# A gated linear attention and a feed-forward layer on one core: one hand-written order of 1,096 steps replaced by another

## The chip, the cores and the metric

The kernel runs on one core of one Trainium2 chip. A core has a matrix engine (TensorE, PE in the profile; its weight loads are PEld), three engines for elementwise work (VectorE or DVE, ScalarE or ACT, GpSimd or POOL) and a queue that issues transfers (SyncE, SP). Each engine runs its own instructions strictly in the order in which they were listed, and waits where an instruction's data or buffer is not ready. [...] The metric is the device time in microseconds (us) of one execution, smaller being better.

## What is computed

Attention with a decaying state over 4 batches x 8 heads, 768 tokens, head size 48, and then a feed-forward layer over the 3072 tokens of 384 features, with 2048 hidden features:

```python
for t in range(S):
    state = alpha[:, :, t, :, None] * state + np.einsum('bhd,bhe->bhde', k[:, :, t], v[:, :, t])
    y[:, :, t] = np.einsum('bhd,bhde->bhe', q[:, :, t], state)
...
x = np.ascontiguousarray(attn_out.transpose(0, 2, 1, 3)).reshape(B * S, H * D)
...
h = x @ w_in
r = np.maximum(h, 0.0)
g = s * (r * r) + b
return (g @ w_out).astype(np.float32)
```

## The kernel before

The tokens are cut into 24 blocks of 128 (6 for each batch, numbered 0 to 23). A block goes through a fixed row of steps. Each step is a small Python function that records a few instructions on one engine, and a step's name with the block's number, such as `amat 13`, names it in this document:

- `load x n`, `load_w x w` (SyncE): one of the inputs q, k, v, a(lpha) for a block, or for a pair of blocks (0 to 5 come in pairs w = 0, 1, 2). The input buffers hold 8 blocks.
- `ln` (ScalarE), `cum` (TensorE), `ex` (ScalarE): logarithm of alpha, its running sum over the tokens, and the exponentials of the sum and of its negative.
- `km`, `qm` (VectorE): k and q times those exponentials. Then their transposes: for blocks 0 to 7 by `tr` (TensorE, n and 0 for q or 1 for k) and a copy out of PSUM, `cph` or `cp`; for the pairs from 8 on by a transposing transfer, `trd` (SyncE).
- `amat` (TensorE): the products of k and q inside the block, into the two banks `a_ps`; `am` (VectorE): the causal mask on both.
- `vcast`: v in bf16. `ya` (TensorE): masked products times v. `yi` (TensorE): q times the state from the earlier blocks, added into the same bank. `yev`: the result out of PSUM.
- `sp` (TensorE), `t1` (VectorE), `sd` and `sc`: the block's own part of the state, its sum with the carried state, and the sum decayed, once as the operand of the next block's `yi` (`sd`, two instructions) and once as the next carry (`sc`, POOL). From block 6 on the decay factors come through two small transfers, `last_row` and `decay`.
- `xt`, `xev` (up to block 17) or `xtd` (transfer, from 18 on): y transposed, the left operand of the feed-forward layer.
- `mp n u` (TensorE, 12 matmuls): quarter u of the hidden features, into one of the two banks `h_ps`; `rl` (ScalarE): the maximum with 0; `sq` (VectorE): the square.
- `o n u` (TensorE, 4 matmuls): quarter u of the sum for the output, into `o_ps`; `oev`: out of PSUM; `add_bias` (VectorE, blocks 0 to 12, kept in the space of the `w_in` staging) and `store` (SyncE).

The weights come as four transfers each, `load_w_in` and `load_w_out`, and are cast to bf16 by twelve `win i kk e` and five `wout`. `colsum`, `bias_sum` and `bias_row` make the constant row that b adds. `busy 256` is a matmul on constants into `o_ps`, whose result is not used; 78 of them stand in the opening.

Where a step can run on several engines, its last letter says which: a is ScalarE, v VectorE, p POOL (GpSimd); `sd` with s runs on VectorE and reads PSUM directly. The order of everything is one string, `order`, of 1,096 such steps; a loop at the end of the kernel calls them one by one. Nothing plans or reorders behind it: the listing, engine by engine, is the program. A step's place in the listing thus sets what it queues behind on its own engine, and each engine runs ahead of the others as far as data and buffers let it. Banks are handed out in the listing's order too: `mp`, `xt` and two of the `cum` take turns on the two banks of `h_ps`.

The helper that most engine letters go through, and the one for `sd`:

```python
def copy(eng, out, in_):
    if eng == "a":
        nc.scalar.activation(out=out, in_=in_, func=AF.Copy)
    else:
        (nc.vector if eng == "v" else nc.gpsimd).tensor_copy(out=out, in_=in_)
...
(nc.gpsimd if eng == "p" else nc.vector).tensor_tensor(
    out=sd_sb[n % 2][r, :, d], in0=src[r, :, d], in1=bl[r].to_broadcast([48, NP, 48]), op=ALU.mult
)
```

The lines of the profile: L148 and L142 loads, L154 and L159 weights, L198 fillers, L207 `ln`, L227/L230/L241 `cum`, L251/L252 `ex`, L273 `km`, L281 `qm`, L299 `tr`, L343 `amat`, L351 `am`, L366 `yi`, L382/L392 `ya`, L408/L417 `sp`, L432 `xt`, L457/L459 `t1`, L469 `sd`, L475 `sc`, L500 `mp`, L514 `rl`, L521 `sq`, L536 `o` (L564 for block 23), L553/L573 `oev` with the bias, L588 `add_bias`. L313 (ScalarE) and L315 (VectorE, POOL) are the helper `copy`, so `vcast`, `cph`, `yev`, `xev`, `win` and `oev` share them.

Of the kernel before, what the change touches and what calls it, by code (L numbers as in the profile page):

```python
# [14 lines left out]
def kernel(  # L15
# [628 lines left out]
    def win(i, kk, eng):  # L644
# [15 lines left out]
        busy 256; busy 256; busy 256; load_w k 1; busy 256; busy 256; busy 256; km 0; busy 256; busy 256; busy 256;  # L660
        busy 256; busy 256; busy 256; tr 0 1; busy 256; tr 0 0; load_w q 1; busy 256; busy 256; ex 1; km 1; cph 0 0 a;
        busy 256; busy 256; load_w_in 1; load_w_in 0; busy 256; cph 0 1 v; tr 1 1; ln 3; amat 0; cph 1 1 a; qm 1; tr 1 0;
        busy 256; busy 256; busy 256; busy 256; am 0; vcast 1 a; spread; ln 2; cum 2; cph 1 0 a; amat 1; cum 3; load_w v 1;
# [11 lines left out]
        sq 1 0; sq 0 2; ln 5; xev 3 a; tr 4 1; tr 4 0; cp 4; mp 1 3; wout 0 2 v; mp 0 3; rl 1 3; mp 3 3; cum 5; rl 0 3;
        mp 3 0; rl 3 3; ex 5; sd 3 v; wout 2 4 v; o 0 0; wout 4 8 a; o 1 0; wout 8 12 a; colsum 1; km 5; load k 6; tr 5 1;
        qm 5; tr 5 0; sq 2 2; cp 5; o 2 0; sq 1 3; masks; o 2 1; sc 3; rl 3 0; sq 2 3; o 1 1; wout 12 16 v; o 1 2; ln 6;
        load a 7; o 2 2; o 2 3; colsum 2; o 1 3; oev 2 a; sq 3 3; colsum 3; mp 3 1; cum 6; load k 7; sq 3 0; vcast 5 p;
        oev 1 a; amat 4; mp 3 2; load q 7; vcast 6 p; ex 6; o 0 1; o 0 2; rl 3 1; load a 8; sq 0 3; am 4; amat 5; o 0 3;
        qm 6; tr 6 0; sq 3 1; km 6; tr 6 1; load v 7; vcast 4 a; ya 4; am 5; cp 6; yi 4; ya 5; ln 7; sp 4; oev 0 a; sp 5;  # L680
        t1 4; cum 7; yev 4 a; xt 4; xev 4 v; amat 6; am 6; rl 3 2; sq 3 2; ex 7; mp 4 1; rl 4 1; qm 7; o 3 0; mp 4 3;
        mp 4 2; ln 8; sd 4 v; tr 7 0; load a 9; rl 4 3; load v 8; km 7; ya 6; yi 5; yev 6; yev 5 v; tr 7 1; cp 7; sq 4 3;
        rl 4 2; mp 4 0; load q 9; o 3 1; cum 8; rl 4 0; last_row 6; sq 4 0; amat 7; am 7; xt 6; load a 10; o 3 2; vcast 7 a;
        sp 6; xt 5; load q 8; load k 8; ln 9; ex 8; o 3 3; oev 3 v; sq 4 1; load k 9; xev 6; t1 6; km 8; decay 6; cum 9;
# [89 lines left out]
```

## Time and profile before

| | |
|---|---|
| time, median of 3 runs (lowest, highest) | 188.35 us (187.73, 188.7) |
| the profiled execution | 188.45 us, of which 186.7 us are the span from the first to the last instruction |
| busy: PE, PEld, DVE, ACT, POOL | 178.1, 141.9, 143.7, 117.8, 48.7 us |
| mean granted TensorE clock | 0.998 |
| transfers | 35.13 MB in 122162 packets, 92.1% of the 16 engines' span on SyncE's queue |

The page shows one execution. A line such as `L514 ACT ACTIVATE r_sb<-h_ps ... x94 | 55.4, 599 | 33.6 <-PE h_ps L500 25.7` is a group of instructions: line, engine, what is written and read, how many; then busy time in us and the mean of one in ns; then how long the engine was idle just before them and what ended most of that. A row of the chain or of the timeline is start, duration, engine and line; in square brackets stands the idle time of the engine before it and what ended it. A row of a window gives the busy time of each engine in that stretch, then the clock, the DMA engines' share and GB/s.

### The profile page before, as it was taken

What the parts mean: (1) busy time and instruction counts of PE and PEld (TensorE: products, weight loads), DVE (VectorE), ACT (ScalarE), POOL (GpSimd) and SP (SyncE); (2) the same over time, 40 slices, a digit from 0 to 9 for tenths busy, and PEclk for the clock granted to TensorE, in tenths of its full rate; (3) what the DMA queues carried; (4) which work ended last, traced back from release to release, by engine and by line L of the source; (5) the groups of instructions that cost most, each with busy time, mean ns of one, the idle gap of its engine ahead of it and who ended that gap; (6) DMA issues with size and microseconds to landing.
All of it is one profiled execution on the core that took longest, in us unless ns stands there. A gap on an engine that the chain in (4) does not pass through costs nothing.

```text
span 186.7 us, 6037 instructions
## 1 busy us (share of the span) xinstructions
PE 178.1 (95%) x2490; PEld 141.9 (76%) x2490; DVE 143.7 (77%) x307; ACT 117.8 (63%) x246; POOL 48.7 (26%) x69
## 2 busy tenths in 40 slices
PE   6998799999999999999989999999999999999993
PEld 4886589966788887887677688877977786777782
DVE  5369797998888799994899793898976985862551
ACT  2584669876579876795578676767765643244330
POOL 7113532004003847301314710030263191000000
PEclk9999999999999999999999999999999999999999
DMA  6999999999879999899899999898999755247242
GB/s 151 261 292 347 344 259 381 323 199 188 145 147 169 180 177 173 165 195 181 155 178 152 190 158 196 161 189 152 198 135 175 260 100 123 84 99 222 81 154 86
DMA packets 122162, 35.13 MB, mean 188 GB/s; under 512 B 115341, under 2 KB 120589, under 8 KB 122134
## 3 DMA queue, kind: packets, MB, share of 16 engines
q1 hardware_dynamic: 122130, 34.75, 92.1%
q8 instruction: 19, 0.31, 0.7%
q14 instruction: 9, 0.07, 0.1%
q10 hardware_dynamic: 4, 0.00, 0.0%
HBM read 25.20 MB, written 4.76 MB: 160 GB/s over the span
## 4 chain that ended last, share of the span: by engine, by line
PE 79%; issue 5%; DVE 4%; DMA 3%; ACT 2%; POOL 2%; SPq 2%; DVEq 0%; ACTq 0%; POOLq 0%
PE h_ps L500 32%; PE o_ps L536 28%; PE a_ps L343 4%; DMA v_sb<-in_v_dram 3%; PE a_ps L536 3%; PE y_ps L392 2%; SPq L148 2%; PE y_ps L366 2%; PE p_ps L417 1%; PE a_ps L564 1%; PE ct_ps L227 1%; PE h_ps L432 1%; PE ct_ps L299 1%; POOL sc_sb L475 1%; ACT r_sb L514 1%
## 5 line engine op out<-in xcount | busy, mean ns | idle before, releaser
L514 ACT ACTIVATE r_sb<-h_ps 128x512 bf16<-128x512 f32 x94 | 55.4, 599 | 33.6 <-PE h_ps L500 25.7
L500 PE MATMUL h_ps<-xd_all,w_in_bf 128*128 128x128 bf16 x1128 | 75.0, 219 | 1.2 <-ACT xd_all L313 0.6
L500 PEld LDWEIGHTS <-w_in_bf 128*128 128x128 bf16 x1152 | 67.6, 98 | 5.9 <-issue 0.9
L536 PE MATMUL o_ps<-w_out_bf,gt_all 128*128 128x384 bf16 x336 | 63.5, 326 | 0.1
L536 PEld LDWEIGHTS <-gt_all 128*128 128x128 bf16 x368 | 33.3, 98 | 17.7 <-DVE gt_all L521 0.3
L521 DVE TENSOR_TENSOR gt_all<-r_sb 128x512 bf16<-128x512 bf16 x96 | 40.2, 447 | 6.3 <-ACT r_sb L514 6.2
L475 POOL TENSOR_TENSOR sc_sb<-t_sb,blast_all 112x384 f32<-112x384 f32 x16 | 19.9, 1242 | 44.7 <-DVE t_sb L457 14.6
L469 POOL TENSOR_TENSOR sd_sb<-t_sb,blast_all 48x192 bf16<-48x192 f32 x20 | 16.0, 799 | 27.1 <-DMA blast_all<-row_dr 18.3
L281 DVE TENSOR_TENSOR qk_sb<-q_sb,b_pair 128x384 bf16<-128x384 f32 x24 | 13.9, 582 | 5.0 <-DMA q_sb<-in_q_dram 4.3
L273 DVE TENSOR_TENSOR qk_sb<-k_sb,bi_sb 128x384 bf16<-128x384 f32 x24 | 14.6, 612 | 2.3 <-ACT bi_sb L251 2.3
L313 ACT ACTIVATE y_bf<-y_ps 128x384 bf16<-128x384 f32 x20 | 9.8, 492 | 7.9 <-PE y_ps L392 6.1
L198 PE MATMUL o_ps<-mask 128*128 128x256 bf16 x78 | 13.1, 305 | 1.5 <-DVE mask L611 1.5
L351 DVE TENSOR_TENSOR am_a<-a_ps,mask 128x512 bf16<-128x512 f32 x18 | 12.3, 685 | 2.7 <-PE a_ps L343 2.6
L207 ACT ACTIVATE la_sb<-a_sb 128x384 bf16<-128x384 f32 x24 | 12.4, 522 | 2.4 <-DMA a_sb<-in_alpha_dram 1.8
L553 DVE TENSOR_TENSOR out_sb<-o_ps,bias_w 128x384 f32<-128x384 f32 x10 | 5.6, 555 | 10.2 <-PE o_ps L536 10.2
L315 POOL CAST v_bf<-v_sb 128x384 bf16<-128x384 f32 x9 | 6.2, 699 | 25.8 <-DMA v_sb<-in_v_dram 24.9
L351 DVE TENSOR_TENSOR am_b<-a_ps,mask 128x512 bf16<-128x512 f32 x18 | 12.2, 678 | 0.0
L343 PE MATMUL a_ps<-qkT 48*128 48x128 bf16 (+1 forms) x240 | 10.1, 220 | 1.9 <-DVE qkT L315 0.9
L343 PEld LDWEIGHTS <-qkT 48*128 48x128 bf16 (+1 forms) x240 | 6.0, 99 | 6.6 <-issue 4.6
L251 ACT ACTIVATE bi_sb<-ct_ps 128x384 f32<-128x384 f32 x20 | 9.8, 490 | 1.5 <-PE ct_ps L227 1.3
L198 PEld LDWEIGHTS <-mask 128*128 128x128 bf16 x78 | 7.9, 110 | 3.1 <-DVE mask L611 1.5
L469 DVE TENSOR_TENSOR sd_sb<-t_sb,blast_all 48x192 bf16<-48x192 f32 x18 | 8.0, 445 | 2.7 <-DMA blast_all<-row_dr 2.5
(123 smaller groups left out, 214.9 us busy)
## 6 DMA issues: line engine op xcount, KB each, us to landing
a_sb<-in_alpha_dram SPq DMA_DIRECT2D x18, 192.0 KB, 4.5
q_sb<-in_q_dram SPq DMA_DIRECT2D x18, 192.0 KB, 4.4
v_sb<-in_v_dram SPq DMA_DIRECT2D x18, 192.0 KB, 4.0
k_sb<-in_k_dram SPq DMA_DIRECT2D x18, 192.0 KB, 3.4
w_in_st<-in_moe_w_in_dram SPq DMA_DIRECT2D x4, 768.0 KB, 10.8
w_out_st<-in_moe_w_out_dram SPq DMA_DIRECT2D x4, 768.0 KB, 10.4
out_dram<-out_sb SPq DMA_DIRECT2D x10, 192.0 KB, 2.1
out_dram<-w_in_st SPq DMA_DIRECT2D x7, 192.0 KB
```

What stands on the lines that cost most here:

```text
L198: nc.tensor.matmul(out=o_ps[:, 0:n], lhsT=mask4[:, 0], rhs=mask4.rearrange("a p t -> a (p t)")[:, 0:n], start=True, stop=True,)
L207: nc.scalar.activation(out=by_head(la_sb[n % 2][:, :, 0:48], n), in_=by_token(rows("a", n), n), func=AF.Ln)
L273: nc.vector.tensor_tensor(out=by_head(kb_sb[n % 4][:, :, 0:48], n), in0=by_token(rows("k", n), n), in1=by_head(bi_sb[n % 2], n), op=ALU.mult,)
L281: nc.vector.tensor_tensor(out=by_head(qb_sb[n % 4][:, :, 0:48], n), in0=by_token(rows("q", n), n), in1=by_head(b_sb[n % 4][:, :, 0:48], n) ...
L343: nc.tensor.matmul(out=o, lhsT=kT, rhs=qT, start=True, stop=True)
L351: nc.vector.tensor_tensor(out=o, in0=x, in1=m, op=ALU.mult)
L469: (nc.gpsimd if eng == "p" else nc.vector).tensor_tensor(out=sd_sb[n % 2][r, :, d], in0=src[r, :, d], in1=bl[r].to_broadcast([48, NP, 48]) ...
L475: nc.gpsimd.tensor_tensor(out=sc_sb[0:112], in0=t1_sb[0:112], in1=blast[n % 4][0:112].to_broadcast([112, NP, 96]), op=ALU.mult,)
L500: nc.tensor.matmul(out=hp[:, jj * N : (jj + 1) * N], lhsT=w_in_bf[:, kk, 128 * j : 128 * (j + 1)], rhs=xd_sb[g][:, kk, 0:N], start=(kk == ...
L514: nc.scalar.activation(out=rs, in_=h_of.pop((g, u)), func=AF.Relu)
L521: nc.vector.tensor_tensor(out=gt_sb[g][:, u * 512 : (u + 1) * 512], in0=rs, in1=rs, op=ALU.mult)
L536: nc.tensor.matmul(out=op[:, 0:d_model], lhsT=gt_sb[g][:, j * C : (j + 1) * C], rhs=w_out_bf[:, j, :], start=(j == 0), stop=(j == NJ - 1),)
```

## The change

The string `order` is replaced by another one of the same length. It lists the same steps for the same blocks, each once, the 78 fillers included, in another sequence from the first line on; no function is changed. 47 steps have another engine letter: `vcast` of 17 blocks, nine `sd`, six `win`, six `oev`, four `xev`, two `yev`, two `cph`, one `wout` (a few trade places). Counted over the program, VectorE has 301 instructions instead of 307, ScalarE 241 instead of 246, POOL 76 instead of 65, TensorE 2490 and SyncE 155 as before. `sd` of blocks 1, 3, 4, 10, 18 and 22 goes from VectorE to POOL, of 14, 19 and 20 from POOL to VectorE.

The opening, up to the third `amat`, and the end, cut to what the prediction speaks of:

```diff
-        ones m; busy 256; busy 256; busy 256; busy 256; busy 256; busy 256; busy 256; eye; zero qk 1; zero ones_g; upper s;
-        load_w a 0; zero la 1; busy 256; busy 256; zero sd 1; busy 256; busy 256; ones f; scalars; busy 256; busy 256;
...
-        am 1; busy 256; load_w_in 2; busy 256; busy 256; busy 256; busy 256; busy 256; ex 2; km 2; busy 256; busy 256; ex 3;
-        busy 256; qm 2; ya 0; busy 256; busy 256; km 3; busy 256; sp 0; sp 1; t1 0; ya 1; busy 256; busy 256; busy 256;
-        yev 0 v; sd 0 s; tr 2 1; load_w a 2; busy 256; busy 256; busy 256; win 1 0 p; tr 2 0; sc 0; qm 3; win 1 1 a;
-        load_w_in 3; load_w q 2; cph 2 1 a; yi 1; load_w k 2; xt 0; win 1 2 p; xev 0 a; yev 1 a; mp 0 1; win 0 1 p;
-        cph 2 0 v; rl 0 1; t1 1; win 0 0 a; load_w_out 0 4; amat 2; am 2; load_w_out 4 8; busy 256; tr 3 1; busy 256;
-        busy 256; load_w_out 8 12; xt 1; sd 1 v; win 0 2 a; vcast 2 a; busy 256; cph 3 1 v; xev 1 v; tr 3 0; cph 3 0 v;
-        mp 0 0; load_w_out 12 16; rl 0 0; amat 3; mp 1 1; sq 0 1; busy 256; rl 1 1; mp 1 0; vcast 3 p; am 3; win 2 1 a;
...
-        sq 9 0; load q 14; amat 12; rl 10 2; o 8 2; last_row 14; o 8 3; oev 8 a; qm 15; vcast 13 v; sq 9 3; xt 11;
-        load k 16; am 12; amat 13; xev 11; mp 11 3; rl 11 3; sq 9 1; ya 12; load a 17; ln 16; load v 15; sq 10 2; am 13;
...
-        oev 22 a; store 9; store 4; store 11; store 22; o 23 1; rl 23 3; o 23 0; sq 23 3; o 23 2; o 23 3
+        ones m; zero sd 0; busy 256; upper n; busy 256; busy 256; busy 256; busy 256; upper s; load_w a 0; zero blast;
+        scalars; zero sd 1; zero qk 1; busy 256; busy 256; busy 256; busy 256; busy 256; busy 256; busy 256; busy 256;
...
+        busy 256; spread; ex 2; km 2; amat 1; am 1; busy 256; busy 256; busy 256; busy 256; load_w_in 0; vcast 1 p; cum 3;
+        ex 3; tr 2 1; ya 0; ya 1; sp 0; sp 1; yev 0 a; win 0 2 p; busy 256; busy 256; busy 256; busy 256; busy 256;
+        busy 256; km 3; busy 256; cph 2 1 a; xt 0; busy 256; busy 256; busy 256; busy 256; busy 256; busy 256; t1 0;
+        win 0 1 a; sd 0 s; yi 1; yev 1 a; busy 256; sc 0; load_w q 1; busy 256; busy 256; busy 256; xev 0 v; qm 2; t1 1;
+        tr 2 0; cph 2 0 a; tr 3 1; win 0 0 p; xt 1; qm 3; xev 1 a; load_w_in 1; mp 0 0; amat 2; cph 3 1 v; busy 256;
+        busy 256; win 1 0 a; win 1 1 v; busy 256; busy 256; rl 0 0; win 1 2 p; load_w v 1; sd 1 p; tr 3 0; cph 3 0 a;
+        vcast 2 a; vcast 3 p; am 2; mp 1 1; rl 1 1; sc 1; amat 3; sq 0 0; load_w_in 2; busy 256; mp 0 1; rl 0 1; ya 2;
+        win 2 1 a; yi 2; win 2 0 p; win 2 2 a; busy 256; busy 256; am 3; sp 2; sp 3; ya 3; yev 2 a; t1 2; sd 2 v; mp 1 0;
+        rl 1 0; load_w a 2; ln 4; sc 2; busy 256; t1 3; mp 1 2; xt 2; xev 2 v; yi 3; yev 3 v; rl 1 2; cum 4; mp 2 0; ex 4;
+        rl 2 0; load_w k 2; km 4; xt 3; load_w q 2; sc 3; xev 3 v; qm 4; mp 2 1; ln 5; sq 0 1; load_w_in 3; rl 2 1; sq 2 0;
...
+        ex 7; xt 4; xev 4 v; amat 6; o 3 1; load v 6; mp 4 1; am 6; sd 4 p; load q 7; vcast 6 a; rl 4 1; load k 7; qm 7;
...
+        load v 13; vcast 13 p; sp 13; yev 11; xt 11; rl 10 3; km 15; o 8 3; sq 9 2; sq 10 0; trd 12; amat 12; xev 11;
+        decay 12; sc 12; oev 8 a; mp 11 1; rl 11 1; o 9 0; sd 12 p; mp 11 0; load a 16; am 12; rl 11 0; mp 11 2; ya 12;
+        load k 14; last_row 14; qm 15; yev 12; t1 13; amat 13; km 14; load q 14; load k 16; ln 16; o 9 1; o 9 2; qm 14;
...
+        store 16; yi 22; ya 22; decay 22; amat 23; am 23; rl 21 2; sq 20 2; o 19 1; yev 22; xtd 22; o 19 2; o 19 3; sd 22 p;
+        oev 19 a; sq 20 1; yi 23; ya 23; yev 23; sq 20 0; store 18; mp 21 0; store 19; rl 21 0; add_bias 10; store 17;
...
+        store 4; sq 23 3; sq 23 0; sq 23 1; sq 22 3; o 23 0; o 22 3; oev 22 a; o 23 2; o 23 1; store 22; o 23 3
```

More of the change, by code (lines that the diff above doesn't have):

```diff
@@ L660 @@
[L660 to L663, printed above, removed]
-        am 1; busy 256; load_w_in 2; busy 256; busy 256; busy 256; busy 256; busy 256; ex 2; km 2; busy 256; busy 256; ex 3;
@@ L675 @@
[L675 to L684, printed above, removed]
@@ new lines @@
+        rl 5 1; cum 10; km 8; mp 5 3; am 7; sq 5 2; decay 6; sd 6 p; yi 7; mp 6 3; ex 10; sq 4 3; rl 5 3; rl 6 3; sc 6;
+        ya 7; yev 7; sq 6 0; o 4 2; sq 5 1; load k 10; sq 5 3; o 4 3; xt 7; t1 7; sc 7; load v 8; vcast 8 v; km 10;
+        load q 10; sd 7 p; qm 10; mp 6 1; last_row 8; sp 8; colsum 5; xev 7; oev 4 a; mp 6 2; load a 11; ln 11; rl 6 2;
+        o 5 0; o 5 1; o 5 2; rl 6 1; load v 9; cum 11; ex 11; vcast 9 a; trd 8; mp 7 2; amat 8; rl 7 2; decay 8; sq 6 2;
+        load q 11; yi 8; t1 8; o 5 3; load k 11; oev 5 a; am 8; sc 8; sq 6 1; sp 9; sq 6 3; mp 7 1; rl 7 1; colsum 6;
@@ new lines @@
+        o 15 0; am 19; load v 20; load k 20; km 20; sd 19 v; o 15 1; sq 15 3; sq 16 1; yi 19; sc 19; vcast 20 p; store 1;
+        sp 20; load v 22; o 15 2; o 15 3; t1 20; sp 21; ya 19; sq 16 2; mp 17 3; mp 17 0; decay 20; sd 20 v; oev 15 a;
+        o 16 0; rl 17 3; sc 20; load a 22; ln 22; t1 21; cum 22; rl 17 0; load q 23; yev 19; sq 17 3; mp 17 1; rl 17 1;
+        load a 23; ex 22; o 16 1; o 16 2; o 16 3; ln 23; mp 17 2; store 13; rl 17 2; trd 20; amat 20; am 20; cum 23; ex 23;
+        xtd 18; sq 17 0; mp 18 0; mp 18 3; rl 18 0; store 5; sq 17 2; oev 16 a; amat 21; rl 18 3; mp 18 1; sq 17 1; yi 20;
```

113 lines of the change are left out of this document (55 added, 58 removed).

## The prediction

> **What bounds the kernel now.** I read the page first, then busy time by stage, then the chain that ended last, then the timeline of the opening.
>
> ```profile
> span 186.7 us, 6037 instructions
> PE 178.1 (95%) x2490; PEld 141.9 (76%) x2490; DVE 143.7 (77%) x307; ACT 117.8 (63%) x246; POOL 48.7 (26%) x69
> L198 PE MATMUL o_ps<-mask 128*128 128x256 bf16 x78 | 13.1, 305 | 1.5 <-DVE mask L611 1.5
> ```
>
> TensorE counts as busy for 95% of the span. But 78 of its matmuls are `busy` fillers, and a matmul's row is longer than its slot (below, twelve `mp` matmuls leave within 0.67 us). So time is lost in two ways: fillers, which stand where nothing real can run yet, and waits. By stage:
>
> ```profile
> core 0: us, PE busy (x) PEld busy (x) DVE busy (x) ACT busy (x) POOL busy (x), PEclk, DMA share, GB/s
> 0.00:25.00 25.00, 20.61 (x302) 16.91 (x303) 16.40 (x44) 13.52 (x31) 9.29 (x27) 1.00 1.06 281
> 25.00:37.12 12.12, 12.08 (x227) 11.23 (x225) 10.47 (x23) 11.46 (x26) 2.44 (x3) 1.00 1.08 325
> 37.12:89.00 51.88, 51.73 (x732) 40.22 (x730) 45.46 (x88) 39.22 (x81) 15.19 (x15) 1.00 1.06 175
> 89.00:109.00 20.00, 19.05 (x264) 14.69 (x262) 17.87 (x37) 13.59 (x31) 8.21 (x12) 1.00 1.18 171
> 109.00:187.00 78.00, 74.60 (x977) 58.81 (x974) 53.45 (x119) 39.97 (x79) 13.61 (x12) 0.99 0.71 150
> ```
>
> The opening loses 4.4 us of TensorE besides its fillers. After that, idle time is 0.15 us up to 89, 0.95 from 89 to 109, and in the last row only the end behind the last matmul (3.0 us) and 0.4 more. So a new order can win in the opening, a little around 100 us, and nowhere else; it can lose anywhere. The chain through the opening:
>
> ```profile
> 11.31 5.69 issue
> ...
> 17.02 0.61 POOL w_in_bf L315
> ...
> 20.10 0.40 PE a_ps L343 x16
> 20.51 0.45 DVE am_a L351
> ...
> 21.70 0.34 DVE sd_sb L469
> ...
> 22.05 0.35 DVE sd_sb L469
> ...
> 22.44 0.42 DVE qkT L315
> 22.87 0.26 DVE xd_all L315
> 23.13 0.34 DVE qkT L315
> ...
> 23.51 0.42 PE a_ps L343 x16
> ...
> 32.23 0.44 PE o_ps L198 x4
> ...
> 32.83 0.45 PE ct_ps L299 x8
> 33.28 0.67 PE h_ps L500 x12
> ...
> 36.47 0.65 PE o_ps L536 x4
> 37.12 0.65 PE a_ps L536 x4
> ```
>
> Two limits follow each other: the first quarter of `w_in` (17.02), then VectorE, which has five pieces between `am 2` and `amat 3` (23.51). The same rows give prices on TensorE (each a piece of the chain): `mp` 0.67, `o` 0.65, two `tr` 0.45 and a filler 0.11. Everything below is set against 186.7 us of span, in an execution of 188.45; the median of the runs is 188.35, so 0.1 comes off at the end.
>
> **The change, part 1: the opening up to `amat 3`.** Counted in the two listings, the same work stands ahead of `amat 3`: 70 fillers, 4 `cum`, 8 `tr`, 3 `amat`, 2 each of `ya`, `sp`, `xt` and `mp`, one `yi`, the `spread`. So the time at which `amat 3` starts compares directly. It hangs on landings:
>
> ```profile
> 4.68 0.94 ACT L207 ACTIVATE la_sb<-a_sb 128x384 bf16<-128x384 f32 x2 [1.81 <-DMA a_sb<-in_alpha_dram]
> 10.81 0.50 POOL L315 CAST v_bf<-v_sb 128x384 bf16<-128x384 f32 x1 [5.43 <-DMA v_sb<-in_v_dram]
> 17.02 0.61 POOL L315 CAST w_in_bf<-w_in_st 128x512 bf16<-128x512 f32 x1 [5.71 <-DMA w_in_st<-in_moe_w_in_dram]
> w_in_st<-in_moe_w_in_dram SPq DMA_DIRECT2D x4, 768.0 KB, 10.8
> 15.00:20.00 5.00, 3.61 (x68) 2.83 (x66) 3.93 (x9) 1.96 (x4) 2.85 (x4) 1.00 1.08 344
> ```
>
> `v 0` is the fifth load of a pair and 6.13 us behind the first: 1.53 us each. SyncE's queue is in order; the new one is a0 k0 q0 a1 k1 v0, `w_in 0`, q1, `w_in 1`, v1 against a0 k0 q0 a1 v0 k1 q1, `w_in 1`, `w_in 0`, v1. So `v 0` lands at 12.3 (it was 10.8), harmless, since `ya 0` must wait for `am 0` until about 13.7. The first quarter took 17.02 - (4.68 + 6 x 1.53) = 3.2 us, so `w_in 0` lands at 15.5, q1 at 17.0 (was 13.9), and the second quarter, whose predecessors are the same set in both orders, at 17.02 + 0.786 MB (768 KB) / 344 GB/s, the last column of the row of 15 to 20 us, = 19.3.
>
> Followed with those: `qm 2` waits for q1 (17.0 + 0.6), `tr 2 0` 17.7, its copy on ScalarE to 18.4, `mp 0 0` beside it to 18.8, `amat 2` 18.8 (was 20.10). Behind it VectorE first has `win 1 1`, which waits for 19.3. A cast of that size has no row on VectorE; ScalarE and POOL take 0.6, and 128x384 takes VectorE 0.35 at 91.74 (timeline), so 0.35 to 0.6; I take 0.4, nearest its own smaller row. Then `am 2`, 1.3 us (two tiles), to 21.0, and `amat 3` at 21.2, against 23.51: **-2.3 us**. The five pieces that stood there in before (1.71 us in the chain) are gone from this place: `sd 1` is on POOL, `cph 3 0` on ScalarE, `cph 3 1` and `xev 1` ahead of `am 2` or on ScalarE. If the second quarter lands 1 us later, the gain is 1.3; if it does not hold `am 2` up, 2.7.
>
> **Part 2: `amat 3` to `o 1 0`** (at 37.12, so 13.61 us in before). The new listing has one `mp`, one `o` and two `tr` more ahead of `o 1 0`: 0.67 + 0.65 + 0.45 = 1.77 us more work done by then, with the same 78 fillers. It also has new waits: `sp 2` directly behind `am 3` (0.4), and `mp 2 1`, which needs the bank of `rl 2 0`, queued on ScalarE behind `ex 4` (0.8); the old ones here, 0.6, go. So 0.6 net: `o 1 0` starts at 21.2 + 13.61 + 1.77 + 0.6 = 37.2, no earlier, but 1.77 us further in the work. **Gain so far 1.7.** `w_in 3`, after k2 and q2 now, and `w_out` close the same set of bytes; the casts of `w_out` are queued behind `rl`s later than they land.
>
> **Part 3: `o 1 0` to the end.** The same operations, so what counts is cover: TensorE work listed between a producer and its consumer. The largest loss in before:
>
> ```profile
> L514 ACT ACTIVATE r_sb<-h_ps 128x512 bf16<-128x512 f32 x94 | 55.4, 599 | 33.6 <-PE h_ps L500 25.7
> 93.71 0.21 PE L343 MATMUL a_ps<-qkT 48*128 48x128 bf16 x1 [0.28 <-DVE am_a L351]
> 94.31 0.38 PE L343 MATMUL a_ps<-qkT 48*128 48x128 bf16 x7 [0.39 <-DVE am_b L351]
> 91.74 0.35 DVE L315 CAST v_bf<-v_sb 128x384 bf16<-128x384 f32 x1
> ```
>
> `amat 13` waits for `am 12`, which VectorE starts after `vcast 13` and a square. Now `vcast 13` is on POOL and three `mp` and an `o` (2.66 us) stand between `amat 12` and `amat 13`, so this goes. Like it go the short covers of `ya 14` (one `o` pair) and `sp 15`. Counting starts rather than ends, before loses 1.95 us in the stretch of 89 to 109; new short places are `mp 16 3` and `mp 15 1`, where four `rl`-sized steps of ScalarE (0.60 each by the row, 0.5 from start to start) are queued under 1.4 and 2.0 us of cover. I take 1.95 - 0.75: **-1.2 us**, with -2.5 and +0.5 as ends (all small gaps close; the new ones are deeper).
>
> **Part 4: other queues.** SyncE issues the same 155 transfers. The transposes `trd` now have 10.3 to 12.3 us of cover ahead of their first user instead of 9.0 to 10.9; `xtd 20` and `xtd 21` have less (5.7 and 6.3 instead of 6.6 and 9.8), `xtd 22` and `23` more: nothing. VectorE issues six instructions fewer (301), ScalarE five fewer, POOL eleven more: six halves of `sd`, four `vcast`, one `win`. On VectorE and ScalarE that is slack, costed at nothing, since TensorE sets the pace there. On POOL the rows are:
>
> ```profile
> L469 POOL TENSOR_TENSOR sd_sb<-t_sb,blast_all 48x192 bf16<-48x192 f32 x20 | 16.0, 799 | 27.1 <-DMA blast_all<-row_dr 18.3
> L469 DVE TENSOR_TENSOR sd_sb<-t_sb,blast_all 48x192 bf16<-48x192 f32 x18 | 8.0, 445 | 2.7 <-DMA blast_all<-row_dr 2.5
> L469 POOL TENSOR_TENSOR sd_sb<-t_sb,blast_all x20: 497/540/2604, 61.5 to 151.3; 48x192 bf16<-48x192 f32 x20
> 148.76 5.17 POOL L469 TENSOR_TENSOR sd_sb<-t_sb,blast_all 48x192 bf16<-48x192 f32 x2 [3.74 <-DVE t_sb L459]
> 149.07 1.02 DVE L281 TENSOR_TENSOR qk_sb<-q_sb,b_pair 128x384 bf16<-128x384 f32 x2
> ```
>
> A pair of `sd` costs 1.6 us on POOL instead of 0.9, and `yi` of the next block waits for it. The tightest: `sd 22` before `yi 23` has 2.65 us of TensorE work listed behind `sp 22`, of which `t1` takes 0.75: 1.9 left for 1.6. `sd 4` has 2.3 left, `sd 1` about 3. Nothing, as long as the pair takes its mean.
>
> The end is alike: three `o 23` pieces behind `oev 22`, one add, one store.
>
> ```profile
> 183.69 0.36 DVE out_sb L573
> ```
>
> **Sum.** 186.7 - 1.7 - 1.2 = 183.8 of span, with 1.75 around it 185.55, less 0.1 for the median: 185.4.
>
> **Rivals.** *POOL is locked out (ends slower).* At 148.76 a pair of `sd` took 5.17 us, over three times its mean, while VectorE ran products of two SBUF operands back to back. If that happens to `sd 22`, `yi 23` is 5.17 - 1.9 = 3.3 us late, `yi 5` 2.9, and `yi 2`, with `vcast 3` and `sp 2` behind it on POOL, 2.2. One such pair takes the forecast to 188.5, no change; two to 191.3, slower. For it: eleven more instructions on POOL, three of them pairs with under 3 us of cover. Against: beside these three VectorE mostly runs `am` and copies, which read PSUM, and in before half of the twenty pieces took 0.54 us or less, with both of the longest in the one pair at 148.76. [...]
>
> *The opening's gain is lost to the transfers.* The DMA share is 1.06 to 1.08 up to 37 us: if TensorE, 1.7 us ahead, only waits longer for the last quarter and `w_out`, part 3 alone is left: 188.35 - 1.2 = 187.2. For it: the same bytes. Against: in before the weights are cast behind other work of their engines, not on landing, from the third quarter on.
>
> *All of it works.* Opening 2.3 and 3.6 of small gaps later: 182.5.
>
> **How the numbers follow.** Forecast 0.42 (185.4, its own range 184.2 to 186.8), all of it 0.13 (182.5), opening lost 0.13 (187.2): all faster, 0.68. One locked pair or the like 0.11 (188.5): no change; a measurement of this kernel cannot tell 0.5%, 0.94 us, from none. Two or more 0.21 (191.3): slower. The range of 182.4 to 190.0 leaves out about 0.05 below and 0.15 above.
>
> **What would show it.** Right: `amat 3` near 21 us directly behind `am_b`; `o 1 0` at about 37 with 15 `mp` done; idle TensorE from 89 to 109 well under 0.95; POOL's busy time near 57 us. Wrong: a wait of `p_ps` or `y_ps` at L366 for `sd_sb` on POOL, pairs there over 3 us, `am_a` waiting for a cast of `w_in` past 20 us, or new waits of `h_ps` for `r_sb` spread over the middle.

## The result and the profile after

The new listing takes 187.36 us in the median of 14 runs (186.02 to 188.5), the old one 188.38 on the same chip (187.49 to 188.98): a ratio of 0.994 (95% interval 0.9917 to 0.9962), 1.0 us faster where 3.0 were forecast. The time lies inside the range. Two later sets of runs on other chips (the second and the third set below), where before takes 189.1, gave 0.998 and 1.002, both with an interval that holds 1: no gain that can be told. The execution that was profiled took 186.14 us, span 184.4, which is nearly the forecast's 183.8; it is the second quickest of the 14. Whoever had only this profile would call the forecast right.

The page of the new listing first (span, busy time, fillers, `sd` on POOL), then its busy time by the stages that the prediction used:

```profile
span 184.4 us, 6035 instructions
PE 176.8 (96%) x2490; PEld 141.9 (77%) x2490; DVE 141.8 (77%) x301; ACT 116.6 (63%) x241; POOL 48.3 (26%) x80
L469 POOL TENSOR_TENSOR sd_sb<-t_sb,blast_all 48x192 bf16<-48x192 f32 x26 | 15.7, 604 | 49.1 <-DVE t_sb L459 25.7
L198 PE MATMUL o_ps<-mask 128*128 128x256 bf16 x78 | 12.4, 298 | 1.5 <-DVE mask L611 1.5
```
```profile
0.00:25.00 25.00, 21.89 (x361) 18.19 (x361) 16.97 (x44) 15.71 (x35) 12.15 (x31) 1.00 1.06 269
25.00:37.12 12.12, 11.98 (x190) 11.18 (x188) 9.93 (x23) 11.11 (x22) 3.97 (x6) 1.00 1.04 339
37.12:89.00 51.88, 51.54 (x730) 40.38 (x728) 46.34 (x91) 38.35 (x80) 12.88 (x17) 1.00 0.99 167
89.00:109.00 20.00, 19.82 (x285) 15.98 (x284) 15.32 (x34) 13.71 (x30) 7.49 (x9) 1.00 1.04 178
109.00:187.00 78.00, 71.56 (x934) 56.16 (x932) 53.21 (x113) 37.68 (x77) 11.85 (x19) 0.99 0.79 155
```

TensorE works 1.28 us more in the first 25 us (21.89 against 20.61), and its idle time from 89 to 109 fell from 0.95 to 0.18. `sd` on POOL got shorter in the mean (604 ns against 799). The opening's timeline, rows of POOL, VectorE and TensorE:

```profile
12.14 1.15 POOL L315 CAST v_bf<-v_sb 128x384 bf16<-128x384 f32 x2 [6.75 <-DMA v_sb<-in_v_dram]
14.13 0.88 POOL L315 CAST w_in_bf<-w_in_st 128x512 bf16<-128x512 f32 x1 [0.84 <-DMA w_in_st<-in_moe_w_in_dram]
16.85 0.56 DVE L281 TENSOR_TENSOR qk_sb<-q_sb,b_pair 128x384 bf16<-128x384 f32 x1 [0.76 <-DMA q_sb<-in_q_dram]
17.47 0.43 PE L299 MATMUL o_ps<-ident,qk_sb 128*112 128x128 bf16 x4 [0.68 <-DVE qk_sb L281]
18.93 0.43 DVE L315 CAST w_in_bf<-w_in_st 128x512 bf16<-128x512 f32 x1 [0.25 <-DMA w_in_st<-in_moe_w_in_dram]
18.89 0.42 PE L343 MATMUL a_ps<-qkT 48*64 48x128 bf16 x16
19.96 0.68 DVE L351 TENSOR_TENSOR am_b<-a_ps,maskw 128x512 bf16<-128x512 f32 x1
20.76 0.42 PE L343 MATMUL a_ps<-qkT 48*64 48x128 bf16 x16
```

Nearly the forecast row by row: `v 0` at 12.1 (12.3), q1 16.85 (17.0), `tr 2 0` 17.47 (17.7), the second quarter of `w_in` 18.93 (19.3), its cast on VectorE 0.43 (0.4), `amat 2` 18.89 (18.8), and `amat 3` behind `am_b` at 20.76 (21.2).

So where does a slower execution lose? To compare two listings at one moment, I took TensorE's time less the work it had done by then (each step at its undisturbed slot: `mp` 0.67, `o` 0.65, and so on). The difference between two listings is what one is ahead of the other, in us; before is here its execution of 188.45:

| ahead of before at | 37 us | 89 | 109 | 140 | 160 | last step |
|---|---|---|---|---|---|---|
| new listing, execution of 186.14 | 1.4 | 1.9 | 3.4 | 2.9 | 2.7 | 2.8 |
| new listing, execution of 188.51 (third set) | 1.8 | 2.3 | 3.6 | 2.3 | 0.5 | 0.4 |

Up to 109 us both hold everything that was forecast, and more. What differs lies behind that. Here are the stretches 109 to 140 and 140 to 160 of before, then of the new listing in the third set:

```profile
109.00:140.00 31.00, 31.00 (x441) 24.92 (x439) 25.07 (x55) 22.09 (x46) 5.87 (x6) 1.00 0.97 167
140.00:160.00 20.00, 19.95 (x257) 15.45 (x255) 15.78 (x35) 9.39 (x19) 7.74 (x6) 1.00 0.71 165
```
```profile
109.00:140.00 31.00, 30.50 (x400) 22.98 (x399) 28.38 (x59) 18.84 (x41) 7.57 (x11) 1.00 1.10 171
140.00:160.00 20.00, 18.40 (x250) 14.58 (x247) 10.34 (x23) 10.02 (x20) 2.89 (x5) 1.00 0.89 160
```

1.6 us of TensorE are missing from 140 to 160. The chain of that execution through it, and SyncE's timeline beside it:

```profile
142.52 0.58 SPq L583
...
143.16 0.59 SPq L583
...
143.79 4.03 DMA q_sb<-in_q_dram
...
147.84 0.56 DVE qk_sb L281
...
149.76 3.26 DMA k_sb<-in_k_dram
...
153.05 0.06 DVE qk_sb L273
...
155.60 0.81 PE o_ps L536 x4
```
```profile
137.99 3.18 SPq L306 DMA_TRANSPOSE qkT<-qk_sb  x1
141.26 1.21 SPq L440 DMA_TRANSPOSE xd_all<-y_bf  x1
142.52 1.22 SPq L583 DMA_DIRECT2D out_dram<-w_in_st  x2
143.79 0.59 SPq L142 DMA_DIRECT2D q_sb<-in_q_dram  x1
144.47 2.22 SPq L440 DMA_TRANSPOSE xd_all<-y_bf  x1
146.74 0.59 SPq L142 DMA_DIRECT2D k_sb<-in_k_dram  x1
147.37 1.22 SPq L583 DMA_DIRECT2D out_dram<-w_in_st  x2
148.64 1.08 SPq L580 DMA_DIRECT2D out_dram<-out_sb  x2
149.76 0.46 SPq L142 DMA_DIRECT2D k_sb<-in_k_dram  x1
```

This is the new order of SyncE. Stores of old blocks (L583, L580), which nobody waits for, stand ahead of q 22 and of k 23, which VectorE needs as soon as they land; VectorE stands still, and `sq`, and with it `o 18 0` at 155.60, comes late. `mp 19 1` waits 1.1 us for `xtd 19`. The change itself brought these stores forward. Here are all stores of blocks 0 to 5, two transfers each, in before and then in this execution (shortest, median and longest issue in ns, then the start of the first and of the last in us):

```profile
L583 SPq DMA_DIRECT2D out_dram<-w_in_st x12: 467/593/1262, 157.6 to 179.3; - x12
L583 SPq DMA_DIRECT2D out_dram<-w_in_st x12: 472/589/974, 130.1 to 179.2; - x12
```

Four of the six blocks (1, 5, 0 and 2) are now stored between 130.1 and 152.9 us, in the stretch where TensorE loses; before stored none of them ahead of 157.6. In before SyncE issues `trd 20` at 132.81, 1.2 us after its inputs (VectorE's last `km` and `qm` for it) are ready; here it is 137.99, 3.1 us after them, and the inputs themselves come 3.3 us later than in before, though TensorE is ahead.

### The profile page after: what moved, and what is told of

It is laid out like the page before. It is cut to its first block, busy times and chain, and to the rows that moved or that the text cites. A ratio compares the mean times of both kernels' runs of the same rounds, so it can differ in the third digit from the quotient of the medians.

```text
span 184.4 us, 6035 instructions
## 1 busy us (share of the span) xinstructions
PE 176.8 (96%) x2490; PEld 141.9 (77%) x2490; DVE 141.8 (77%) x301; ACT 116.6 (63%) x241; POOL 48.3 (26%) x80
## 4 chain that ended last, share of the span: by engine, by line
PE 61%; SPq 12%; DVE 12%; DMA 10%; issue 2%; ACT 0%; DVEq 0%
PE o_ps L536 24%; PE h_ps L500 23%; SPq L148 8%; DMA w_out_st<-in_moe_w_out_dram 5%; DMA qkT<-qk_sb 4%; SPq L154 4%; PE a_ps L536 3%; PE a_ps L343 3%; DVE qk_sb L273 2%; DVE gt_all L521 2%; PE y_ps L392 2%; DVE am_b L351 2%; DMA k_sb<-in_k_dram 2%; DVE qk_sb L281 2%; DVE w_in_st L588 1%
## 5 line engine op out<-in xcount | busy, mean ns | idle before, releaser
L521 DVE TENSOR_TENSOR gt_all<-r_sb 128x512 bf16<-128x512 bf16 x96 | 39.7, 450 | 5.3 <-ACT r_sb L514 5.3
L475 POOL TENSOR_TENSOR sc_sb<-t_sb,blast_all 112x384 f32<-112x384 f32 x16 | 16.6, 1034 | 18.7 <-DVE t_sb L459 12.6
L315 POOL CAST v_bf<-v_sb 128x384 bf16<-128x384 f32 x13 | 8.1, 628 | 39.0 <-DMA v_sb<-in_v_dram 38.8
L273 DVE TENSOR_TENSOR qk_sb<-k_sb,bi_sb 128x384 bf16<-128x384 f32 x24 | 14.1, 590 | 5.1 <-ACT bi_sb L251 4.5
L351 DVE TENSOR_TENSOR am_a<-a_ps,mask 128x512 bf16<-128x512 f32 x18 | 12.3, 683 | 6.4 <-PE a_ps L343 6.1
L281 DVE TENSOR_TENSOR qk_sb<-q_sb,b_pair 128x384 bf16<-128x384 f32 x24 | 14.6, 613 | 1.0 <-DMA q_sb<-in_q_dram 0.8
L198 PE MATMUL o_ps<-mask 128*128 128x256 bf16 x78 | 12.4, 298 | 1.5 <-DVE mask L611 1.5
L313 ACT ACTIVATE y_bf<-y_ps 128x384 bf16<-128x384 f32 x21 | 10.3, 492 | 5.1 <-issue 2.3
L252 ACT ACTIVATE b_pair<-ct_ps 128x384 f32<-128x384 f32 x20 | 9.9, 496 | 0.0
L313 ACT ACTIVATE xd_all<-h_ps 128x384 bf16<-128x384 bf16 x13 | 6.4, 494 | 4.9 <-PE h_ps L432 4.9
```

The lines of the kernel that those rows point to most:

```text
L198: nc.tensor.matmul(out=o_ps[:, 0:n], lhsT=mask4[:, 0], rhs=mask4.rearrange("a p t -> a (p t)")[:, 0:n], start=True, stop=True,)
L273: nc.vector.tensor_tensor(out=by_head(kb_sb[n % 4][:, :, 0:48], n), in0=by_token(rows("k", n), n), in1=by_head(bi_sb[n % 2], n), op=ALU.mult,)
L281: nc.vector.tensor_tensor(out=by_head(qb_sb[n % 4][:, :, 0:48], n), in0=by_token(rows("q", n), n), in1=by_head(b_sb[n % 4][:, :, 0:48], n) ...
L351: nc.vector.tensor_tensor(out=o, in0=x, in1=m, op=ALU.mult)
L475: nc.gpsimd.tensor_tensor(out=sc_sb[0:112], in0=t1_sb[0:112], in1=blast[n % 4][0:112].to_broadcast([112, NP, 96]), op=ALU.mult,)
L521: nc.vector.tensor_tensor(out=gt_sb[g][:, u * 512 : (u + 1) * 512], in0=rs, in1=rs, op=ALU.mult)
```

## The experiments

Theory T: the transfers are a second bound just behind TensorE, and the new order of SyncE's steps spends what the new order of the others gains. Its rival T2: it is the transfers' bytes and not their order. Theory F: TensorE's late speed-up in the opening (at 4.3 us in the execution of 186.14, at 6.4 in the third set's; last section) makes the spread. Other rivals: the engines' letters, POOL, an unlucky draw. Each set of runs was made on one chip, with runs of before beside it; ratios are to those.

**The new listing again**, on two more chips (the second and the third set). No edit.

> The changed kernel once more, nothing edited. It stands at 187.36 us in the median, though the execution that was profiled took 186.14 and its span (184.4) is the forecast's (183.8) within 0.6. Theory A, the forecast's mechanism is right and the profiled execution was one of the quick ones: the times spread again from about 186.0 to 188.5 with a median near 187.3, and a profile of a slower execution shows its extra 1 to 2 us in one or a few stretches, at instructions that wait for a transfer. Rival B, the first 14 times were a wide draw and the median belongs near 186: this time the median is under 186.5.

> The new listing unedited, beside the two with SyncE's steps moved. It stood at 0.994 and 0.998 of before in two calls. Theory T: 0.993 to 1.0 again, with a spread of 2.5 to 3.5 us; both edited ones under it by 1 us or more.

Measured: 189.11 (ratio 0.998, 0.9945 to 1.001) and 189.22 (1.002, 0.9988 to 1.0049), from 187.2 and 188.1 upward. Rival B falls: the quick profile was the exception. Theory A's median near 187.3 was missed too, by 1.8 us: the first set itself, at 0.994, was the quickest of the three.

**Less to move.** Both listings with half of the heads in every load from block 8 on.

```diff
-        (eng or nc.sync).dma_start(out=dst.rearrange(pattern, h=H), in_=tokens)
+        nh = H // 2 if n >= 8 else H
+        (eng or nc.sync).dma_start(out=dst.rearrange(pattern, h=H)[:, 0:nh], in_=tokens[:, 0:nh])
```

> The new listing with every load from block 8 on bringing half of its heads (the other half of the buffer keeps older values, so the output is not the reference's; all other work is the same): 6.3 MB less to move. Theory T: with room on the transfers TensorE sets the pace, and against before's listing with the same loads this one gains what the forecast summed, 2.5 to 3.2 us. Rival (the loss is TensorE's or another engine's): the difference between the two stays at 0 to 1 us.

> Before's listing with the same halved loads from block 8 on (the output is not the reference's). Theory T: before had more time between issue and use, so it gains little from the room, 0 to 0.7 us, and the changed kernel's counterpart gains 1.5 to 3. Rival: both gain the same.

Measured: new listing 185.68 (0.9811, 0.9776 to 0.9846; all six times within 0.6 us), before's 188.11 (0.995, 0.9922 to 0.9977). With room on the transfers the new listing is 2.4 us ahead, a little under the 2.5 to 3.2 expected, and its spread is gone. Before gains too, 1.0 us where 0 to 0.7 was expected: it was already held a little by its transfers. The new listing's two stretches with half the loads:

```profile
109.00:140.00 31.00, 30.70 (x410) 23.75 (x409) 28.73 (x59) 18.73 (x42) 7.28 (x11) 1.00 0.66 121
140.00:160.00 20.00, 20.00 (x282) 16.19 (x280) 13.56 (x28) 11.48 (x22) 3.28 (x5) 1.00 0.65 124
```

The DMA share falls from 1.10 to 0.66 and TensorE is full from 140 to 160. SyncE issues a transpose `trd` in 1.9 us in the mean, where it takes 3.3 (execution of 186.14) and 3.5 (third set) with all loads, and it reaches all eight within 0.1 us of their inputs. This settles that the missing gain went to the transfers. Whether to their bytes or their order, the next ones tell.

**A few of SyncE's steps moved.** SyncE's part of the listing, from 129 us on; nothing else changes:

```diff
- load k 20; store 1; load v 22; decay 20; load a 22; load q 23; load a 23; store 13; trd 20; xtd 18; store 5; load q 22;
- xtd 19; load k 22; store 0; store 14; store 15; load k 23; xtd 20; store 2; load v 23; trd 22;
...
+ load k 20; load v 22; decay 20; load a 22; load q 23; load a 23; trd 20; xtd 18; store 13; load q 22;
+ xtd 19; load k 22; load k 23; store 14; store 15; xtd 20; load v 23; trd 22;
...
+ xtd 23; store 2; store 0; store 5; store 1; store 9;
```

> The new listing with six steps of SyncE moved: stores 2, 0, 5 and 1 behind xtd 23, store 13 behind xtd 18, k 23 behind k 22. (The kernel of the earlier trial of this had other moves than its text says: k 22, k 23 and v 23 ahead of store 13, so ahead of trd 20, and the four stores ahead of decay 22; it took 193.8, of which yi 23 lost 3.9 us to decay 22 and 2.5 to the half clock behind.) Theory T: 0.3 to 1.2 us faster than the changed kernel, since trd 20 and xtd 19 are issued 1 us earlier. Rival T2: no change within 0.3%.

> The new listing with six steps of SyncE moved, once more, beside the unedited one in the same call. Theory T: again 1 to 2.5 us under the unedited new listing, ratio to before 0.98 to 0.99. Rival: six quick draws; no more than 0.5 us under the unedited one.

Measured: 187.04 (0.9844, 0.9788 to 0.99) and, beside the unedited listing on the same chip, 187.31 (0.9874, 0.9828 to 0.9921) against 189.22. Six steps of a queue that carries no arithmetic give 1.9 us, more than the 0.3 to 1.2 that was expected first, and the result is faster than both kernels. The stretch 140 to 160 of the second of these:

```profile
140.00:160.00 20.00, 19.85 (x262) 15.70 (x260) 13.02 (x28) 11.65 (x23) 3.60 (x5) 1.00 0.74 147
```

19.85 us of work instead of 18.40, with k 23 issued at 144.5 instead of 149.8. From 109 to 140 that execution lost 2.2 us, 1.5 of it at `amat 16` and `amat 18`, which wait for their transposes, so this stretch is still short of transfers.

The kernel of a first trial has other moves than its text says: k 22, k 23 and v 23 stand ahead of `store 13`, and the four stores ahead of `decay 22`.

> The new listing with seven of SyncE's steps moved and nothing else: stores 1, 5, 0 and 2 behind xtd 21, store 13 behind xtd 18, k 23 behind k 22. In the slow profiled execution of the new listing mp 19 1 lost 1.95 us and o 18 0 0.54 behind this stretch, in the quick one 0.19 and 0.1. Theory T: 0.3 to 1.2 us faster than the changed kernel. Rival (those losses were one execution's): no change within 0.3%.

Measured: 193.81 (1.028, 1.0236 to 1.0325). As a test of its own text it is void; as a price it is plain. SyncE's timeline has the four stores as eight transfers, and `decay 22` behind them (L267):

```profile
158.73 5.09 SPq L583 DMA_DIRECT2D out_dram<-w_in_st  x8
...
165.05 1.78 SPq L267 DMA_DIRECT2D blast_all<-row_dr  x1
```

`decay 22` lands at 168.8, the `sd` pair and `yi 23` wait for it, and TensorE stands for 3.9 us: four misplaced stores cost that, and 2.5 us more (last section).

**SyncE in order of need**, by the users' times in the profile of the new listing; the third trial's queue, from 41 us on, beside the new listing's:

```diff
- load a 9; load v 6; load q 7; load k 7; load a 8; load q 9; load q 8; last_row 6; load v 7; load a 10; load k 9; load k 8;
- decay 6; load k 10; load v 8; load q 10; last_row 8; load a 11; load v 9; trd 8;
+ load v 6; load q 7; load k 7; load a 9; load a 8; load v 7; load q 8; load q 9; load k 9; load a 10; load k 8; last_row 6;
+ load v 8; load k 10; decay 6; load a 11; load q 10; load v 9; load k 11; load q 11; ... trd 8;
```

Four trials: from q 6 on (35 us) with two faults, the same with one fault mended, with both mended, and from q 13 on (76 us). In the first two and in the one with fewer fillers beside them, `decay 18` had slipped ahead of `sc 15`, which then read another block's decay: that part of the computation is changed there.

> The new listing with SyncE's steps from q 6 on (35 us) put in the order in which they are needed (each load, transpose and decay by its user's time, the stores of blocks 0 to 12 behind the transpose of block 22); every other step keeps its place. Theory T, the queue of transfers is the second bound and the new listing's order of it costs the missing 1 to 2 us: the median falls by 1 to 2 us against the changed kernel, toward the ratio 0.985, with gaps ahead of amat 12, mp 19 1 and o 18 0 gone. Rival F alone (the spread comes from the opening): no change within 0.3%.

> As the run with SyncE's steps in order of need, but with v 2 of the windowed loads left where it is: there it had slipped from 31 to 44 us, and TensorE lost 5 us at 46 to 51 waiting for blocks 4 and 5, while behind 55 us the gaps ahead of amat 12, mp 19 1 and o 18 0 were gone. Theory T: without that slip the kernel comes to 185.5 to 187, 1 to 2.5 us under the changed kernel's 188 to 189 of this chip, with a spread under 2 us. Rival: issuing loads earlier lengthens the queue ahead of the transposes and gives the gain back; no change within 0.3%.

> The new listing with SyncE's steps from q 6 on in order of need, with two faults of the earlier trials mended: v 2 stays in its place, and decay 18 stays behind sc 15. (In those trials sc 15 read the decay that decay 18 brought, so that part of the computation was changed, and it waited 8.6 us for it; yi 17 came 1.9 us late and the granted clock fell to half for 3.4 us behind that, 3.6 us together.) The trial without the first fault stood at 189.9. Theory T, the order of the transfers is what costs the new listing its gain: 186 to 187, below the changed kernel and below before's 188.9. Rival T2, it is the bytes and not their order: 188 to 189.5, no better than the changed kernel.

> The new listing with SyncE's steps in order of need from q 13 on (76 us) and unchanged ahead of that. In the run with the order of need from 35 us on, the transposes from block 12 on were issued 0.06 us after their inputs (1.2 to 2.6 in the new listing) and the gaps behind 90 us came to 1.7, but trd 8 was held 4.8 us behind loads that had been pulled ahead, and amat 8, o 7 0 and yi 10 lost 3.4. Theory T: without that, 186 to 187.5 and a ratio to before of 0.982 to 0.99. Rival T2 (bytes, not order): 188 to 189.5.

Measured: 191.38 (1.0108, 1.0064 to 1.0152), 189.89 (1.0041, 1.0015 to 1.0067), 188.88 (0.9949, 0.9906 to 0.9992) and 188.23 (0.9929, 0.9902 to 0.9957). None reached what Theory T gave, and the last two lie in the band of 188 to 189.5 that T2 gave (bytes, not order). In the third, the transposes of blocks 12 to 22 were issued 0.06 us after their inputs and no gap over 0.5 us was left behind 90 us, but loads pulled ahead held up `trd 8` by 4.8 us, and three gaps at 68 to 82 us took 3.4. In the fourth `amat 16` and `amat 18` lost 3.7; SyncE reached their transposes 4.1 and 4.6 us late. My order by deadlines, made from one quick profile, moved the shortage about and did not remove it: here the early loads delayed other transfers, and only stores, which have no near user, were moved back for nothing.

**The parts alone.** The new listing up to `o 1 0` with before's order of what is left behind it, and the reverse. Behind the cut they read:

```diff
- o 1 0; o 1 1; colsum 2; wout 8 12 a; colsum 3; o 0 1; cp 5; load a 6; ln 6;
+ o 1 0; load a 6; load q 6; load v 6; load_w v 2; sq 0 2; rl 3 3; wout 8 12 a; load k 6; cp 5; o 2 1;
...
- o 1 0; wout 8 12 a; colsum 1; km 5; load k 6; tr 5 1; qm 5; tr 5 0; sq 2 2; cp 5; o 2 0;
+ o 1 0; masks; sc 3; rl 3 0; colsum 1; km 5; qm 5; mp 3 1; rl 3 1; sq 2 2; sq 1 3; sq 3 0;
```

> The new listing up to and with o 1 0 (about 37 us), then before's order of what is left. Forecast's terms: the opening alone is worth 1.7 us, so 186.7. Theory A with thin lead of the loads as the cause of the spread (after 40 us the new listing gives the loads 0.5 to 4 us less between issue and use than before's): this kernel keeps before's later order, so its times spread like before's (about 1.5 us from lowest to highest). Rival C, the spread comes from the opening (the weights' transfers): this kernel spreads over 2.5 us and its median is near 187.4.

> Before's listing up to and with o 1 0, then the new order of what is left. Forecast's terms: the middle alone is worth 1.2 us, so 187.2. Theory A with thin leads: the loads of the later listing are used 1.4 us later than in the changed kernel, so part of the spread goes, and the gain is 0.3 to 1.2 us (187.2 to 188.1). Rival C: it spreads like before (1.5 us) at 187.2. A third way: the later order loses against before's by itself, 188.5 or more.

Measured: 188.82 (1.0016, 0.9988 to 1.0044) and 190.57 (1.01, 1.0052 to 1.0148). By itself the opening gives nothing and the rest costs 1%, so the two terms of the sum do not add. In the first, TensorE is 1.5 us ahead at 37 us and loses that again, and more, at `o 8 1`, `amat 12` and `amat 16`, 2.9 us together, the last two for transposes. It does so with before's own order of transfers behind `o 1 0`, the stores of blocks 0 to 2 and 5 from 158.8 us on as in before: with a DMA share of 0.99 to 1.07 from 37 to 140 us this lead was lost without the new order too. In the second, SyncE stands 4.9 us before its first `last_row`, which needs the exponentials of blocks 6 and 7, and it reaches the transposes of blocks 12 to 20 1.6 to 3.4 us after their inputs.

**The engines back.** The new listing with before's letters: all 47 (its text says 45), or those of blocks 6 to 23 alone.

```diff
- vcast 6 a; ... sd 10 p; ... vcast 13 p; ... sd 18 p; ... sd 22 p;
+ vcast 6 p; ... sd 10 v; ... vcast 13 v; ... sd 18 v; ... sd 22 v;
```

> The new listing with every cast, eviction and state product back on the engine that it has in before (45 pieces). The forecast costed the moves at nothing except in the opening, where sd 1, cph 3 0 and xev 1 leave VectorE ahead of am 3 (about 1 us of it): so 186.5 to 188.4 by the forecast's own reading, set against the 187.36 of the changed kernel. Rival D, the new letters cost time by POOL's slow pairs and are what eats the gain: this kernel is faster than the changed one by 0.5 us or more (under 186.9). Theory E, order and letters were made for each other: slower than 188.4.

> The new listing with the engines of before for the 25 casts, evictions and state products of blocks 6 to 23 that changed; the opening keeps its new ones. With all 45 back it took 196.1, 7 us more, with SyncE's first last_row held 5.96 us and the transfers starved there. Theory T: most of the 7 us comes from the opening's letters (late ex 7, queue starved), so this stays within 2 us of the changed kernel. Rival E: the later letters carry it, each short spot of VectorE and ScalarE costs a little; 3 to 6 us slower. Rival D, POOL's slow pairs: faster than the changed kernel.

Measured: 196.12 (1.0384, 1.0352 to 1.0416) and 191.32 (1.013, 1.01 to 1.0161). Rival D (POOL) falls: the new letters as a whole help, the moves to POOL among them; these were not tried alone. The late letters are worth 2 to 3.6 us (1.3% over before, against the new listing's -0.6 to 0.2%), the others nearly 5. The second kernel's windows show where:

```profile
109.00:140.00 31.00, 27.28 (x357) 20.53 (x355) 26.12 (x54) 18.16 (x39) 6.10 (x10) 1.00 1.10 175
```

27.28 us of TensorE in 31, lost in six gaps of 0.58 to 1.13 us and smaller ones. There `sd 18`, `vcast 18` and `vcast 21` are on VectorE again; which of the letters does it was not tried. In the first, SyncE's timeline has 5.96 us of nothing ahead of `last_row 6` (L262):

```profile
45.70 1.91 SPq L142 DMA_DIRECT2D q_sb<-in_q_dram  x2
53.57 0.31 SPq L262 DMA_DIRECT2D row_dr<-b_pair  x1
```

**Fewer fillers.** 8 of the 25 ahead of `cum 1` left out, in the new listing and in the second and third order of need.

```diff
- busy 256; load_w k 0; busy 256; busy 256; busy 256; busy 256; zero la 1; upper i; load_w q 0; table; ln 1; zero b 1;
- busy 256; zero ones_g; ones f; busy 256; busy 256; ones g; cum 1;
+ load_w k 0; zero la 1; upper i; load_w q 0; table; ln 1; zero b 1;
+ zero ones_g; ones f; ones g; cum 1;
```

> The new listing with 8 of the 25 fillers ahead of cum 1 left out (the other 70 stay). In the two profiled executions of the new listing the first fillers leave 0.213 us apart, and later ones 0.109, and the step from one to the other comes at 4.3 us in the first and not before 7 in the second: cum 1 starts at 5.61 and at 6.83. Theory F, the spread of the new kernel comes in part from there: with 17 fillers cum 1 starts at about 5.1 in either case, amat 3 0.5 to 1.1 us earlier than in the changed kernel, and the spread of the times falls by about 1 us. What reaches the end is 0.5 to 1.1 us if TensorE alone sets the end, and under 0.3 if the transfers set it further on (theory T). Rival: the fillers taken away are what speeds TensorE up; then the fast pace comes later and nothing is gained, or up to 1 us lost.

> The same with the 8 fillers ahead of cum 1 left out as well. Theory F with T: with room on the transfers the earlier start of the opening reaches the end, 0.3 to 0.8 us under the run without this. Rival: the weights' landings (w_out at 33 us) take it, difference under 0.3.

> The first of these with 8 of the 25 fillers ahead of cum 1 left out as well. Theory F with T: 0.3 to 0.8 us under the first. Rival: the same within 0.3, since w_out's landing at 33 us takes what the opening gains.

Measured: 188.76 (0.9961, 0.993 to 0.9992), 191.44 (1.0135, 1.0093 to 1.0178) and 188.74 (0.9933, 0.9901 to 0.9966; without the change 0.9949). `cum 1` starts at 5.1 to 5.2 us as expected, and no gain that these intervals can tell reaches the end; the times of the first still spread from 187.34 to 191.12. Theory F explains differences at `amat 3`, but not the time; and with halved loads the spread vanished although the fillers were all there. Why the second is 1.5 us above its partner is open.

## Why the prediction was wrong

- *What bounds the kernel* was half right. The view of TensorE was read well; but the same windows showed a DMA share of 1.06 to 1.18 up to 109 us, and that second bound was quoted and then used for the opening alone.
- *Part 1* was right: `amat 3` at 20.76 for 21.2, every landing but one within 0.4 us (the first quarter of `w_in` came at 14.1, not 15.5), and VectorE's wait for the second quarter was where it was put. In the third set's execution it was 21.38.
- *Part 2* was right: `o 1 0` at 37.33 and 36.88 for 37.2, 1.4 and 1.8 us ahead for 1.7.
- *Part 3* was right in kind and a little small: between 37 and 109 us the new listing wins 1.8 to 2.0 where 1.2 was put for all that is left; 1.3 to 1.5 of it come from 89 to 109, where before loses 1.95. The 0.75 taken off for `mp 16 3` and `mp 15 1` did not come: neither waits over 0.1 us in the two executions.
- *Part 4* is the step that failed: it put the transfers at nothing ("SyncE issues the same 155 transfers"). The same transfers, needed earlier and issued in another order on a queue whose share is 0.97 to 1.11 up to 140 us, are not nothing. Behind 109 us the lead falls by 0.6 us in the quick execution and by 3.2 in the third set's (3.4 ahead at 109 down to 2.8 at the end, 3.6 down to 0.4). Bounded by runs: 2.4 us of gain with room on the transfers, where 1.0 to -0.1 remain without. I had counted the cover of the transposes in listed TensorE work, as if SyncE were free when their inputs are ready; in the new listing's profile it reaches those of blocks 12, 14, 16 and 20 1.2 to 2.6 us late, in before's none over 1.2. Two things are in this step. One is the full queue by itself: with before's order of transfers behind `o 1 0` the opening's lead of 1.5 us was lost as well. The other is the new order, which brings stores forward and so the loads and transposes that are needed soon back: moving six steps gave 1.9 us back. How the rest divides between the two is open; the new listing with the whole of before's order of transfers was not run.
- In the same part the letters on VectorE and ScalarE were "slack, costed at nothing". For the sum that did no harm, but the reason was wrong: put back as before has them, the late ones cost 2 to 3.6 us.
- *POOL locked out* did not happen in the profiled execution: the longest single `sd` there took 1.19 us. Hence POOL's busy time of 48.3 us, not 57. That VectorE's products hold POOL up was not shown: the profile of before has the pair of 5.17 us and the products beside each other, and no run tried them apart.
- *The opening's gain is lost to the transfers* gave 187.2 and came nearest to 187.36. Its mechanism was the right one in the wrong place: not `w_in` and `w_out` before 37 us, but loads and transposes from 109 to 160. That the median came so near to its number is luck.
- *The end* was put as alike; from the last add (181.27 in the new listing, 184.05 in before) to the end of the span it is 3.1 us instead of 2.65.

## What to carry to other kernels

Where the transfers' share stands near 1 in a window (0.97 to 1.11 here up to 140 us), price the order of the queue as you price an engine: for each transfer, what is ahead of it on the queue and how soon its user comes. Stores belong behind the steps that somebody waits for; moving six steps, five of them stores, gave more here than the new order of a thousand steps, while pulling loads ahead by need gave nothing that could be told. A gain upstream of a second bound can be only lent (here a lead of 1.5 us at 37 us that did not reach the end): test it with that bound relieved (here half the loads) before believing a sum, and take the median of many times on more than one chip, not the one profile, for the result.

## What the runs showed that I had not expected

In the profiles TensorE's fillers start at half of their later pace (0.213 us from one to the next, then 0.109), and the moment of the change lies 2.1 us apart in two executions of the new listing. The first rows of TensorE's timeline, the execution of 186.14 and then the third set's:

```profile
1.52 4.25 PE L198 MATMUL o_ps<-mask 128*128 128x256 bf16 x25 [1.52 <-DVE mask L611]
5.61 0.41 PE L230 MATMUL y_ps<-la_sb,Ui_bf 128*128 128x192 bf16 x3
```
```profile
1.52 5.27 PE L198 MATMUL o_ps<-mask 128*128 128x256 bf16 x25 [1.52 <-DVE mask L611]
6.63 0.41 PE L230 MATMUL y_ps<-la_sb,Ui_bf 128*128 128x192 bf16 x3
```

The same 25 matmuls take 1.02 us longer: the switch comes at 4.3 us in the one and, worked out from the two paces, at 6.4 in the other. The windows show a granted clock of 1.00 from the start in both, but in the first of them the trace's record of that clock begins only at 4.32 us, so that the 1.00 says nothing of the time before. In the profile of before the pace doubles at 5.1 us and the record begins at 5.15; in the second set's it does not double before 7 us, with 7 matmuls started in each microsecond from 4 to 7 and 13 in the next. From the earliest to the latest of these four that is 2.7 us, though the first filler leaves at 1.52 in all. What sets the moment was not shown.

Behind two stalls late in the kernel the granted clock fell to 0.50, for 6 us and for 3.4 us. In the first trial of the moved stores, windows of 2 us behind its stall (the number ahead of the DMA share is the granted clock):

```profile
168.00:170.00 2.00, 0.00 (x0) 0.00 (x0) 1.56 (x4) 0.00 (x0) 1.02 (x2) 0.89 0.65 166
170.00:172.00 2.00, 1.61 (x22) 1.61 (x22) 0.75 (x1) 0.49 (x1) 0.34 (x1) 0.50 0.49 179
172.00:174.00 2.00, 2.00 (x19) 1.83 (x17) 0.00 (x0) 0.81 (x2) 0.00 (x0) 0.50 0.25 49
174.00:176.00 2.00, 2.00 (x8) 0.90 (x7) 0.76 (x2) 0.38 (x1) 0.00 (x0) 0.50 0.76 254
```

After 3.9 us of standing still TensorE works at half clock (0.50) from 170.4 to 176.4, for 6 us, and four steps take 0.58 to 0.63 us too long each. In the second order of need a stretch of 4 us in which it was still busy for half of the time (2.07 us) was followed by half clock too, for 3.4 us (worked out from the means of 0.59 in the last row and 0.56 in the 2 us behind it):

```profile
126.00:128.00 2.00, 1.19 (x20) 0.96 (x18) 1.09 (x3) 0.98 (x2) 1.28 (x2) 1.00 1.85 152
128.00:130.00 2.00, 0.88 (x15) 0.64 (x15) 2.00 (x6) 0.00 (x0) 0.55 (x2) 1.00 0.57 124
130.00:132.00 2.00, 2.00 (x20) 1.87 (x19) 1.06 (x3) 0.23 (x1) 1.50 (x3) 0.59 0.96 194
```
